# Prologue and first lots of a linear-attention and feed-forward kernel: another order of loads, scores and masks, narrower products of zeros, and the lower part of lot 4 placed sooner

## The chip, the cores and the metric

The kernel runs on one core of a Trainium2 chip. The metric is the device time of one execution in microseconds (us).

## The reference, cut to what matters

Linear attention with decay, in blocks of 64 tokens, over 4 batches, 8 heads, 768 tokens and 64 features; then a feed-forward network with a squared ReLU on the 3072 tokens of 512 features.

```python
for b in range(nb):
    qb, kb, vb = (q[:, :, sl], k[:, :, sl], v[:, :, sl])
    intra = np.einsum('bhic,bhjc->bhij', qb, kb) * Dmask[None]
    intra = np.einsum('bhij,bhjd->bhid', intra, vb)
    inter = np.einsum('bhid,bhde->bhie', qb * lam_pow[None], kv_state)
    out[:, :, sl] = intra + inter
    kv_state = lam_block * kv_state + np.einsum('bhsd,bhse->bhde', kb * rev_pow, vb)
...
h = x @ w_in
g = np.maximum(h, 0.0) ** 2
return g @ w_out
```

## The kernel before, in words

**Tiling.** Tokens are taken in 24 chunks of 128 (`t`), four of which make a group of 512 (`m`). For a chunk, `scores(t)` multiplies k and q of all heads into two PSUM tiles, `masked(t)` (VectorE, DVE) multiplies them with the decay mask into `a`, `news(t)`, `faded(t)` and `update(t)` carry the state `kv`, and `within(t)` and `before(t)` sum the chunk's output in PSUM. `split(t)` stores it as an upper part `xh` (ScalarE, ACT) and a lower part `xl` (DVE, the closure kept in `low[t]`). `prep_k(t)` and `prep_q(t)` scale k and q in place on GpSimd (POOL), with columns of the mask and with the powers `qpow`.

**Feed-forward.** For each of 16 slices `f` of the inner dimension, `hidden(m, f)` is 12 products into one PSUM bank: four of `wh` with `xh`, four of `wl` with `xh`, four of `wh` with `xl`. `square` (ACT) makes `gh`, `rest` (DVE) makes `gl`, and `project(m, f)` adds to four accumulators, for each of them a product of `gh` with `wh`, one of `gh` with `wl` and one of `gl` with `wh`. `project` of slice `f` is issued behind `hidden` of slice `f + 1`.

**Lots.** The weights come from memory as raw 64-bit words in 17 lots, counted from 0; lot `u` holds slice `u` of `w_in` and slice `u − 1` of `w_out`. A lot is loaded into `raw` (two buffers), then `first_hi(u)` (ACT) makes `A`, `first_lo(u)` (ACT) scales the low words in place, `clamp`, `shift`, `sign` and `rounded` (DVE) finish `A`, `upper(u)` (ACT) casts it to `wh`, and `lower(u)` (DVE) subtracts to `wl`. `A` too has two buffers. The load of lot `u + 2` waits until `rounded(u)` has read the buffer. `hidden(0, f)` needs lot `f`, `project(0, f)` lot `f + 1`. `turn` is a one-element copy on POOL that orders the work there.

**Order.** The order on each engine is written by hand: an engine runs its instructions as the program lists them. TensorE (PE) starts with products of zeros (L63 and L65, the second loop `PHASE = 7` products of 128 columns, each 2 records in the trace), then the masks' products (`get_mask`, L253), scores of chunk 0, the powers' products (`get_qpow`, L266), scores of chunk 1, and `news(0)`. The masks' products fill two banks of the pool `ps_h`; `halves[0]` (ACT) and `halves[1]` (DVE) copy them to the mask. Loads go through SyncE's queue (SP) in the order of the program; lot 2 through ACT's.

**The loop.** From `new_x(1)` on the loop over `f` issues, for each slice, `hidden(0, f)`, DVE's work on lot `f + 2`, `lower(f + 1)`, the load of lot `f + 4`, `square`, `rest`, ACT's work on lot `f + 3`, and one step of the attention of the next group: `scores(t)` at `f % 4 == 0`, `masked(t)` at 1, `attend(t)` (news, within, before, update, split) at 2.

Lines in the trace: L80 and L89 the loads of q, k and v; L115 the load of a lot; L120 `first_hi`; L125 `first_lo`; L133 `clamp`; L137 `shift`; L144 `sign`; L150 `rounded`; L156 `upper`; L159 `lower`; L259 the mask's copies; L285 `scores`; L298 `prep_k`; L292 `prep_q`; L304 `masked`; L319 `news`; L327 `within`; L334 `before`; L353 the addition to `kv`; L361 and L362 `xh` and `xl`; L523 `hidden`; L530 to L533 `square`; L538 `gl`; L553, L554 and L558 `project`.

Of the kernel before, what the change touches and what calls it, by code (L numbers as in the profile page):

```python
# [15 lines left out]
P = 128  # L16
# [9 lines left out]
G = 4  # L26
# [5 lines left out]
NLOT = NF + 1  # L32
# [3 lines left out]
def body(ctx: ExitStack, tc: tile.TileContext, qT, kT, kvq, lam, w, out):  # L36
    nc = tc.nc
# [5 lines left out]
    ps_acc = ctx.enter_context(tc.tile_pool(name="ps_acc", bufs=G, space=PSUM))  # L43
    ps_h = ctx.enter_context(tc.tile_pool(name="ps_h", bufs=2, space=PSUM))
# [11 lines left out]
    kv = const.tile([P, NPR, P], F32, name="kv")  # L56
# [4 lines left out]
    w_ = ps_a.tile([P, DM], F32, name="att")  # L61
    for n in (NPR, NPR, 2):
        nc.tensor.matmul(w_[:, 0 : n * P], kv[:, 0, :], kv[:, 0:n].rearrange("p a b -> p (a b)"), start=True, stop=True)  # L63
    for n in range(PHASE):
        nc.tensor.matmul(w_[:, 0:P], kv[:, 0, :], kv[:, 0, 0:P], start=True, stop=True)  # L65


    feat, tok, lent = {}, {}, {}
# [1 line left out]
    def load_qk(t):  # L70
        if t in (2, 3):
            lent[t] = wk.tile([P, 2, KT * C, 2], F32, name=f"lent{t}", tag=("xh", "xl")[t - 2])
            x = lent[t][:, 0].rearrange("p a b -> p (a b)")
        elif (t, 0) in lent:
            x = lent[t, 0]
        else:
            x = io.tile([P, 2 * DM], F32, name="qk_sb")
        feat[t] = x.rearrange("p (k a b) -> p k a b", k=2, a=NPR)
        for k, y in enumerate((kT, qT)):
            nc.sync.dma_start(out=feat[t][:, k], in_=y[t])  # L80

    def load_kv(t):
        if t in (2, 3):
            x = lent[t][:, 1].rearrange("p a b -> p (a b)")
        elif (t, 1) in lent:
            x = lent[t, 1]
        else:
            x = io.tile([P, 2 * DM], F32, name="kv_sb")
        nc.sync.dma_start(out=x, in_=kvq[t, :, 0 : 2 * DM])  # L89
        x = x.rearrange("p (k h d) -> p k h d", k=2, h=H)  # L90
        tok[t] = x[:, 0], x[:, 1]
# [8 lines left out]
    def lot(t, u):  # L100
        if u in (0, NF):
            return t[:, u : u + 1]
        return t.rearrange("p (s f) d -> p s f d", s=2)[:, :, u]

    def pieces(u):
        return [x for x in ((0, u), (1, u - 1)) if 0 <= x[1] < NF]
# [3 lines left out]
    def wload(u, engine=nc.sync):  # L110
        if u < NLOT:
            x = pieces(u)
            raw[u] = wk.tile([P, len(x) * DM], I64, name="raw", tag="raw")
            for i, (side, f) in enumerate(x):
                engine.dma_start(out=raw[u][:, i * DM : (i + 1) * DM], in_=w[side, :, f])  # L115
# [7 lines left out]
    def first_lo(u):  # L123
        L = cv[u][0]
        nc.scalar.activation(L, L, AF.Copy, scale=2.0**-29)  # L125

    def first(u):
        first_hi(u)
        first_lo(u)

    def clamp(u):
        A = cv[u][2].bitcast(F32)
        V.tensor_scalar(out=A, in0=A, scalar1=2.0**-15, scalar2=float(LIM), op0=ALU.max, op1=ALU.min)  # L133

    def shift(u):
        A = cv[u][2]
        V.tensor_scalar(  # L137
            out=A, in0=A, scalar1=3, scalar2=0x3FFFFFFF,
            op0=ALU.logical_shift_left, op1=ALU.bitwise_and,
        )  # L140

    def sign(u):
        L, Hw, A = cv[u]
        V.scalar_tensor_tensor(  # L144
            out=A, in0=Hw, scalar=0xC0000000, in1=A, op0=ALU.bitwise_and, op1=ALU.bitwise_or
        )

    def rounded(u):
        L, Hw, A = cv[u]
        V.tensor_tensor(out=A, in0=A, in1=L, op=ALU.add)  # L150

    def whole(u):
        return cv[u][2].bitcast(F32).rearrange("p (a d) -> p a d", d=DM)
# [4 lines left out]
    def lower(u):  # L158
        V.tensor_tensor(out=lot(wl, u), in0=whole(u), in1=lot(wh, u).bitcast(F32), op=ALU.subtract)  # L159
        cv.pop(u)  # L160

    def turn(u, half):
        x = cv[u][2].bitcast(F32)[0:1, 0:1] if half else wl[0:1, u, 0:1].bitcast(F32)
        nc.gpsimd.tensor_copy(mark[:, 0:1], x)

    wload(0)
    for t in (0, 1):
        load_qk(t)
        load_kv(t)
    load_qk(2)  # L170
    wload(1)
# [36 lines left out]
    for j in range(2):  # L208
# [5 lines left out]
        lambda o, x, y, op=op: V.tensor_tensor(out=o, in0=x, in1=y, op=op)  # L214
# [5 lines left out]
    b_, t_, u_, c_, d_, af = (sq[:, i, 0 : NS - 1] for i in range(6))  # L220
# [28 lines left out]
    def get_mask():  # L249
        half = [ps_h.tile([P, DM], F32, name="h") for _ in range(2)]  # L250
        nb = DM // P
        for b in range(2 * nb):
            nc.tensor.matmul(  # L253
                half[b // nb][:, b % nb * P : (b % nb + 1) * P], pz[:, b * T : b * T + C], one,
                start=True, stop=True, skip_group_check=True,
            )
        m = mask.rearrange("k j p (e b i) -> k (j p) e b i", e=2, i=T)
        return [
            lambda copy, e=e: copy(m[:, :, e], half[e].rearrange("k (b c i) -> k c b i", b=nb, i=T))  # L259
            for e in range(2)  # L260
        ]
# [18 lines left out]
    def scores(t, pool, name):  # L280
        sc_of[t] = [pool.tile([P, DM], F32, name=name) for _ in range(2)]
        k_, q_ = feat[t][:, 0], feat[t][:, 1]
        for p in range(NPR):
            for j, r in enumerate(rows):
                nc.tensor.matmul(  # L285
                    sc_of[t][j][:, p * C : (p + 1) * C], k_[r, p], q_[r, p],
                    start=True, stop=True, skip_group_check=True,
                )

    def prep_q(t):  # L290
        if t % NCB:
            nc.gpsimd.tensor_tensor(out=feat[t][:, 1], in0=feat[t][:, 1], in1=qpow, op=ALU.mult)  # L292
# [7 lines left out]
    def masked(t):  # L300
        a_of[t] = []
        for j in range(2):
            a = wk.tile([P, NPR, C], F32, name="a", tag="gl" if t in (1, 3) else "a")
            V.tensor_tensor(  # L304
                out=a, in0=sc_of[t][j].rearrange("p (a b) -> p a b", a=NPR),
                in1=mask[:, j], op=ALU.mult,
            )
            a_of[t].append(a)
# [267 lines left out]
    def new_x(m):  # L576
        xs_of[m] = [wk.tile([P, KT, N], F32R, name=n, tag=n) for n in ("xh", "xl")]
# [418 lines left out]


    new_x(0)
    halves = get_mask()
    first(0)  # L1000
    for op in (clamp, shift, sign):
# [1 line left out]
    halves[0](nc.scalar.copy)  # L1003
    halves[1](V.tensor_copy)
    rounded(0)
    scores(0, ps_acc, "acc")
    get_qpow()
    scores(1, ps_acc, "acc")
    prep_k(0)
    prep_k(1)  # L1010
    prep_q(1)
    masked(0)
    o, u, low = {}, {}, {}

    def att(t, pool, name):
# [9 lines left out]
    masked(1)  # L1025
    lower(0)
    first(1)
    scores(2, ps_h, "h")
    prep_q(2)
    prep_k(2)  # L1030
    att(1, ps_acc, "acc")
# [45 lines left out]
    for f in range(NF):  # L1077
        t, step, u_ = G + f // 4, f % 4, f + 2
        h = hidden(0, f, *xs_of[0])
        if f < 3:  # L1080
            if f < 2:
                lower(u_ - 1)
            clamp(u_)
            shift(u_)
            if f == 2:
                lower(u_ - 1)
            if f == 1:
                turn(u_, True)
                masked(t)
            sign(u_)  # L1090
            if f != 1:
                rounded(u_)
        else:
            if u_ < NLOT:
                for op in (clamp, shift, sign):
                    op(u_)
            if f > 3:
                upper(u_ - 1)
            lower(u_ - 1)
            if u_ - 1 < NF:  # L1100
                turn(u_ - 1, False)
            if u_ < NLOT:
                rounded(u_)
        wload(u_ + 2)
        if f == 3:
            low[G]()
        if f == 0:
            decay(3)
        if step == 0 and f or f == 1:
            prep_k(t)  # L1110
        if step == 1:
            prep_q(t)
        if step == 3:
            if t < 2 * G - 1:
                decay(t)
            else:
                fade_state(False)
        gh = square(h)
        rest(0, f, h, gh)
        if f == 1:  # L1120
            rounded(u_)
        if step == 1 and f > 1:
            masked(t)
        if f < 3:
            if f == 1:
                first_hi(u_ + 1)
            upper(u_)
            if f != 1:
                first_hi(u_ + 1)
        if step == 2:  # L1130
            low[t] = attend(t, ps_a, "att")
            if t > G:
                low[t]()
        if u_ + 1 < NLOT:
            if f >= 3:
                first_hi(u_ + 1)
            first_lo(u_ + 1)
        if prev is not None:
            project(*prev)
        prev = (0, f)  # L1140
        if step == 2:
            load_qk(t + 2)
            load_kv(t + 2)
        if step == 0:
            scores(t, ps_a, "att")
        if f == NF - 2:
            fold_mask()
            scale_k(t + 1)
        if f == NF - 1:
            open_half(t + 1)  # L1150
            scale_k(t + 2)
# [30 lines left out]
    for f in range(NF):  # L1182
        t = first_t + f // 2
        h = hidden(1, f, *xs_of[1])
# [53 lines left out]
    for f in range(NF):  # L1238
        t = first_t + f // 2
# [97 lines left out]
```

## Time and profile before

| what | value |
|---|---|
| time, median of 3 runs | 583.58 us (583.03 to 583.8) |
| time of the profiled execution | 583.46 us |
| its span, first to last instruction | 581.7 us |
| PE busy | 572.8 us, 98% of the span |
| DVE busy | 415.1 us, 71% |
| ACT busy | 272.4 us, 47% |
| POOL busy | 99.2 us, 17% |

The profile is one execution. Times in its rows are us from the start of the span; the time of the execution has 1.76 us more around the span. Busy shares are means over the whole span, and a stage can have another limit than the mean shows. A row of the time line gives start, busy time, engine, line, operation, output and inputs, and how many instructions it merges; in square brackets stands the idle time of the engine before it and what ended it.

### The profile page before, as it was taken

What the parts mean: (1) busy time and instruction counts of PE and PEld (TensorE: products, weight loads), DVE (VectorE), ACT (ScalarE), POOL (GpSimd) and SP (SyncE); (2) the same over time, 40 slices, a digit from 0 to 9 for tenths busy, and PEclk for the clock granted to TensorE, in tenths of its full rate; (3) what the DMA queues carried; (4) which work ended last, traced back from release to release, by engine and by line L of the source; (5) the groups of instructions that cost most, each with busy time, mean ns of one, the idle gap of its engine ahead of it and who ended that gap; (6) DMA issues with size and microseconds to landing.
All of it is one profiled execution on the core that took longest, in us unless ns stands there. A gap on an engine that the chain in (4) does not pass through costs nothing.

```text
span 581.7 us, 12568 instructions
## 1 busy us (share of the span) xinstructions
PE 572.8 (98%) x5020; PEld 485.6 (83%) x5020; DVE 415.1 (71%) x684; ACT 272.4 (47%) x501; POOL 99.2 (17%) x106
## 2 busy tenths in 40 slices
PE   9998999999999999999999999999999999999996
PEld 7986888888888888888888887888788888999996
DVE  5999999942788666786666668687645446997933
ACT  3777877725455556433333334444524234551510
POOL 4421222332322231000000013455000000000000
PEclk9999999999999999999999999999999999999999
DMA  8856576324689695566666645632297766776863
GB/s 300 333 176 242 157 277 217 111 74 145 223 294 373 226 302 181 173 193 198 197 199 199 199 162 168 233 116 71 77 322 231 191 194 186 246 215 204 287 206 106
DMA packets 69386, 119.32 MB, mean 205 GB/s; under 512 B 6352, under 2 KB 30928, under 8 KB 69328
## 3 DMA queue, kind: packets, MB, share of 16 engines
q1 hardware_dynamic: 66864, 115.37, 61.5%
q10 hardware_dynamic: 2464, 3.15, 1.5%
q8 instruction: 40, 0.66, 0.4%
q14 instruction: 18, 0.15, 0.1%
HBM read 88.08 MB, written 29.36 MB: 202 GB/s over the span
## 4 chain that ended last, share of the span: by engine, by line
PE 87%; DVE 8%; ACT 3%; issue 1%; DMA 0%; SPq 0%; DVEq 0%; POOL 0%; ACTq 0%; POOLq 0%
PE h L683 18%; PE h L523 12%; PE acc L553 9%; PE acc L558 8%; PE acc L554 8%; PE acc L931 8%; PE att L683 7%; PE att L931 4%; PE att L444 3%; PE h L931 2%; DVE sums L214 1%; PE h L411 1%; PE att L327 1%; PE att L63 1%; DVE rec L214 1%
## 5 line engine op out<-in xcount | busy, mean ns | idle before, releaser
L553 PE MATMUL acc<-wh,gh 128*128 128x512 f32 x256 | 101.1, 395 | 0.0
L558 PE MATMUL acc<-wh,gl 128*128 128x512 f32 x256 | 99.8, 390 | 0.0
L554 PE MATMUL acc<-wl,gh 128*128 128x512 f32 x256 | 99.8, 390 | 0.0
L683 PE MATMUL h<-wh,ring 128*128 128x512 f32 x320 | 85.8, 390 | 0.0
L530 ACT ACTIVATE h<-h 128x512 f32<-128x512 f32 x48 | 28.0, 583 | 103.6 <-PE h L523 45.8
L683 PEld LDWEIGHTS h<-wh,ring 128*128 128x128 f32 x320 | 59.9, 188 | 13.1 <-DVE kv_sb L214 0.4
L538 DVE TENSOR_TENSOR gl<-h,gh 128x512 fp32r<-128x512 f32 x48 | 32.9, 686 | 39.7 <-ACT h L533 39.7
L553 PEld LDWEIGHTS acc<-wh,gh 128*128 128x128 f32 x256 | 48.0, 188 | 10.9 <-issue 0.5
L558 PEld LDWEIGHTS acc<-wh,gl 128*128 128x128 f32 x256 | 48.1, 188 | 10.5 <-DVE gl L538 0.3
L554 PEld LDWEIGHTS acc<-wl,gh 128*128 128x128 f32 x256 | 48.1, 188 | 9.7
L683 PE MATMUL h<-wl,ring 128*128 128x512 f32 x160 | 49.3, 389 | 0.0
L395 POOL TENSOR_TENSOR kv_sb<-kv_sb,mask 128x512 f32<-128x512 f32 x13 | 16.0, 1229 | 126.0 <-DMA kv_sb<-in_kvq 125.9
L523 PE MATMUL h<-xh,wh 128*128 128x512 f32 x128 | 36.0, 403 | 0.5 <-DVE a L214 0.2
L523 PE MATMUL h<-xh,wl 128*128 128x512 f32 x128 | 34.5, 391 | 1.5 <-DVE wl L159 1.5
L512 POOL TENSOR_TENSOR kvd<-kv,qpow 128x256 f32<-128x256 f32 x27 | 22.3, 826 | 77.9 <-DVE kv L214 63.5
L683 PEld LDWEIGHTS h<-wl,ring 128*128 128x128 f32 x160 | 30.0, 188 | 6.3
L931 PE MATMUL acc<-folds,wh 128*128 128x256 f32 x192 | 35.2, 283 | 0.0
L523 PE MATMUL h<-xl,wh 128*128 128x512 f32 x128 | 34.2, 389 | 0.0
L683 PE MATMUL att<-wh,ring 128*128 128x512 f32 x128 | 34.2, 389 | 0.0
L214 DVE TENSOR_TENSOR wl<-sums,wh 128x1024 fp32r<-128x1024 f32 x24 | 29.2, 1218 | 1.9 <-ACT wh L903 1.9
L931 PEld LDWEIGHTS acc<-folds,wh 128*128 128x128 f32 x192 | 30.0, 192 | 0.0
L523 PEld LDWEIGHTS h<-xh,wl 128*128 128x128 f32 x128 | 23.9, 188 | 7.1 <-DVE wl L159 1.9
(253 smaller groups left out, 1197.0 us busy)
## 6 DMA issues: line engine op xcount, KB each, us to landing
ring<-ws SPq DMA_DIRECT2D x112, 256.0 KB, 3.0
folds<-wt SPq DMA_DIRECT2D x64, 256.0 KB, 3.7
raw<-in_w SPq DMA_DIRECT2D x30, 512.0 KB, 4.3
kv_sb<-in_kvq SPq DMA_DIRECT2D x19, 512.0 KB, 5.5
ws<-parts SPq DMA_DIRECT2D x32, 256.0 KB, 4.4
qk_sb<-in_kT SPq DMA_DIRECT2D x20, 256.0 KB, 4.2
qk_sb<-in_qT SPq DMA_DIRECT2D x20, 256.0 KB, 4.5
out_x<-o SPq DMA_DIRECT2D x16, 256.0 KB, 5.1
```

The lines of the kernel that those rows point to most:

```text
L214: lambda o, x, y, op=op: V.tensor_tensor(out=o, in0=x, in1=y, op=op)
L395: nc.gpsimd.tensor_tensor(out=x, in0=x, in1=y.broadcast_to([P, NPR, 2, D]), op=ALU.mult)
L444: nc.tensor.matmul(o[h][r, p * D : (p + 1) * D], x, y, start=(h, r.start) not in begun, stop=end, skip_group_check=True,)
L512: nc.gpsimd.tensor_tensor(out=kvd, in0=d, in1=qpow[:, :, D - 1 : D].broadcast_to([P, NPR, D]), op=ALU.mult)
L523: nc.tensor.matmul(h, wt[:, f, kt * P : (kt + 1) * P], x[:, kt], start=k == 0, stop=k == 11)
L530: nc.scalar.activation(h, h, AF.Relu)
L538: V.tensor_tensor(out=gl, in0=r, in1=gh.bitcast(F32), op=ALU.subtract)
L553: nc.tensor.matmul(accs[m][i], gh[:, cs], wh[:, j], start=f == 0, stop=False)
L554: nc.tensor.matmul(accs[m][i], gh[:, cs], wl[:, j], start=False, stop=False)
L558: nc.tensor.matmul(accs[m][i], gl[:, cs], wh[:, j], start=False, stop=end)
L683: nc.tensor.matmul(bank, x[:, part_, kt], t[:, q + kt], start=start and z == 0, stop=stop and z == 5, skip_group_check=True,)
L931: nc.tensor.matmul(bank[:, r * 2 * P : (r + 1) * 2 * P], x, y, start=n == 0 and r == 0 and z == 0, stop=n == NQ - 1 and z == 2, skip_group ...
```

## The change

The loads of k and q of chunks 0 and 1 go ahead of lot 0's. The seven products of zeros have 32 columns instead of 128. Scores of chunks 0 and 1 are issued ahead of the masks' products, scores of chunk 2 right behind `masked(0)` instead of behind `first(1)`. In the loop over `f`, `lower(4)` stands ahead of `clamp(5)` at `f = 3`; at `f = 4` and 5 `lower(f + 1)` stands ahead of `sign`; `rounded(5)` and `low[4]` stand behind `rest(0, 3)`; and `first_lo(6)` and `first_lo(7)` move from the end of slices 3 and 4 to the next slice, behind `upper`.

```diff
     for n in range(PHASE):
-        nc.tensor.matmul(w_[:, 0:P], kv[:, 0, :], kv[:, 0, 0:P], start=True, stop=True)
+        nc.tensor.matmul(w_[:, 0:32], kv[:, 0, :], kv[:, 0, 0:32], start=True, stop=True)
...
+    load_qk(0)
+    load_qk(1)
     wload(0)
     for t in (0, 1):
-        load_qk(t)
         load_kv(t)
     load_qk(2)
     wload(1)
...
     new_x(0)
+    scores(0, ps_acc, "acc")
+    scores(1, ps_acc, "acc")
     halves = get_mask()
     first(0)
...
     rounded(0)
-    scores(0, ps_acc, "acc")
     get_qpow()
-    scores(1, ps_acc, "acc")
     prep_k(0)
     prep_k(1)
     prep_q(1)
     masked(0)
+    scores(2, ps_h, "h")
...
     first(1)
-    scores(2, ps_h, "h")
...
         else:
-            if u_ < NLOT:
-                for op in (clamp, shift, sign):
-                    op(u_)
             if f > 3:
                 upper(u_ - 1)
-            lower(u_ - 1)
+                if f < 6:
+                    first_lo(u_)
+            if f == 3:
+                lower(u_ - 1)
+            if u_ < NLOT:
+                clamp(u_)
+                shift(u_)
+                if f in (4, 5):
+                    lower(u_ - 1)
+                sign(u_)
+            if f > 5:
+                lower(u_ - 1)
             if u_ - 1 < NF:
                 turn(u_ - 1, False)
-            if u_ < NLOT:
+            if u_ < NLOT and f > 3:
                 rounded(u_)
         wload(u_ + 2)
-        if f == 3:
-            low[G]()
...
         rest(0, f, h, gh)
-        if f == 1:
+        if f in (1, 3):
             rounded(u_)
+        if f == 3:
+            low[G]()
...
             if f >= 3:
                 first_hi(u_ + 1)
-            first_lo(u_ + 1)
+            if f not in (3, 4):
+                first_lo(u_ + 1)
```

## Rows read from the trace of the kernel before

**Rows 1.** The page's first part: busy time, share of the span and number of instructions of two engines.

```profile
PE 572.8 (98%) x5020; PEld 485.6 (83%) x5020; DVE 415.1 (71%) x684; ACT 272.4 (47%) x501; POOL 99.2 (17%) x106
```

**Rows 2.** The waits of PE and of its weight-load queue (PEld) over the whole span: engine and line, what they waited for, us in total, how often, the longest.

```profile
PE h L523 <- DVE wl L159: 1.5, 1, 1.5
...
PEld acc L558 <- DVE gl L538: 0.3, 1, 0.3
```

**Rows 3.** PE in order of time from 48.5 to 66 us: `hidden(0, 4)`, the start of the projection behind it, `hidden(0, 6)`, and `within(5)` (the last row's window ends before its last product).

```profile
48.56 1.07 PE L523 MATMUL h<-xh,wh 128*128 128x512 f32 x4
51.15 1.19 PE L523 MATMUL h<-xh,wl 128*128 128x512 f32 x4 [1.52 <-DVE wl L159]
...
53.10 0.39 PE L553 MATMUL acc<-wh,gh 128*128 128x512 f32 x1
...
62.80 1.07 PE L523 MATMUL h<-xh,wh 128*128 128x512 f32 x4
...
64.62 1.07 PE L523 MATMUL h<-xl,wh 128*128 128x512 f32 x4
65.61 0.65 PE L327 MATMUL att<-a,kv_sb 128*64 128x128 f32 x7
```

**Rows 4.** DVE in order of time from 45 to 66 us: the additions to `kv`, then `clamp(5)`, `lower(4)`, `rounded(5)`, `low[4]`, `gl(3)`, `clamp(6)`, `clamp(7)` and `masked(5)`.

```profile
45.66 0.86 DVE L353 TENSOR_TENSOR kv<-kvd,att 64x256 f32<-64x256 f32 x2
47.28 0.69 DVE L133 TENSOR_SCALAR A<-A 128x1024 f32<-128x1024 f32 x1 [0.76 <-ACT A L120]
...
49.88 1.22 DVE L159 TENSOR_TENSOR wl<-A,wh 128x1024 fp32r<-128x1024 f32 x1
51.02 1.22 DVE L150 CUSTOM_DVE_ANT_0 A<-raw,A 128x2048 uint16<-128x2048 uint16 x1
52.27 0.69 DVE L362 TENSOR_TENSOR xl<-att,xh 128x512 fp32r<-128x512 f32 x1
52.87 0.68 DVE L538 TENSOR_TENSOR gl<-h,gh 128x512 fp32r<-128x512 f32 x1
53.47 0.68 DVE L133 TENSOR_SCALAR A<-A 128x1024 f32<-128x1024 f32 x1
...
58.93 0.68 DVE L133 TENSOR_SCALAR A<-A 128x1024 f32<-128x1024 f32 x1
...
64.39 1.28 DVE L304 TENSOR_TENSOR a<-att,mask 128x512 f32<-128x512 f32 x2
```

**Rows 5.** First all waits of DVE from 47.3 to 120 us (columns as in rows 2; the 0.8 is the 0.76 of rows 4), then the busy time of each engine from 75 to 120 us (the second number is the stretch's length; at the end the clock, the DMA share and GB/s).

```profile
DVE A L133 <- ACT A L120: 1.2, 2, 0.8
...
75.00:120.00 45.00, 45.00 (x281) 36.65 (x281) 43.97 (x55) 34.21 (x46) 14.15 (x15) 1.00 0.53 178
```

**Rows 6.** ACT in order of time from 45 to 66 us: `upper(4)`, `first_hi(5)`, the last step of `square` of slice 3, and `first_hi(7)`.

```profile
45.18 1.05 ACT L156 CAST wh<-A 128x1024 fp32r<-128x1024 f32 x1 [1.25 <-DVE A L150]
46.13 1.12 ACT L120 ACTIVATE A<-raw 128x1024 f32<-128x1024 f32 x1
...
49.79 0.59 ACT L533 ACTIVATE h<-h 128x512 f32<-128x512 f32 x1
...
57.35 1.17 ACT L120 ACTIVATE A<-raw 128x1024 f32<-128x1024 f32 x1 [1.48 <-DVE wl L159]
```

**Rows 7.** The load issued between 52.6 and 52.8 us, the second half of lot 7: its size and us from issue to landing.

```profile
raw<-in_w SPq DMA_DIRECT2D x1, 512.0 KB, 4.6
```

**Rows 8.** PE at the start: the first product of zeros and the second record; then the records of the seven products, in three windows (from the first one on, from 6.87 on, from 7.69 on: the number behind x falls as the window begins later); last, from the list of instructions on `qk_sb`, the score products with the least, median and greatest ns of one.

```profile
1.38 1.22 PE L63 MATMUL att<-kv 128*128 128x512 f32 x1 [1.38 <-POOL pz L189]
...
2.39 1.06 PE L63 MATMUL att<-kv 128*128 128x512 f32 x1
...
5.81 2.38 PE L65 MATMUL att<-kv 128*128 128x128 f32 x14
...
6.87 1.31 PE L65 MATMUL att<-kv 128*128 128x128 f32 x9
...
7.69 0.50 PE L65 MATMUL att<-kv 128*128 128x128 f32 x3
...
L285 PE MATMUL acc<-qk_sb x32: 272/272/373, 9.9 to 13.0; 64*128 64x128 f32 x32
```

**Rows 9.** The prologue. PE in order of time: masks' products, scores of chunk 0, powers' products, `news(0)`. Then the busy time of each engine (PE, PEld, DVE, ACT, POOL) from DVE's mask copy at 10.01 to `lower(1)` at 26.16; the two `prep_k` on POOL (least, median and greatest ns); and two loads with us from issue to landing: q of chunk 0, issued between 2.6 and 2.7 us, and the second half of lot 2, issued by ACT at 18.4.

```profile
8.02 1.95 PE L253 MATMUL h<-pz 128*128 128x128 f32 x16
9.90 1.16 PE L285 MATMUL acc<-qk_sb 64*128 64x128 f32 x16
10.99 1.15 PE L266 MATMUL att<-pz,odd 8*128 8x128 f32 x8
...
13.17 0.69 PE L319 MATMUL att<-kv_sb 128*64 128x64 f32 x16
...
10.01:26.16 16.15, 16.15 (x299) 14.99 (x300) 13.92 (x19) 9.75 (x20) 9.13 (x7) 1.00 0.91 346
...
L298 POOL TENSOR_TENSOR kv_sb<-kv_sb,mask x2: 1051/1241/1431, 10.8 to 12.2; 128x512 f32<-128x512 f32 x2
...
qk_sb<-in_qT SPq DMA_DIRECT2D x1, 256.0 KB, 4.4
...
raw<-in_w ACTq DMA_DIRECT2D x1, 512.0 KB, 6.8
```

## The prediction

> **What bounds the kernel now.** I read the page first: PE is busy 572.8 us of the 581.7 us span, DVE 415.1 [rows 1]. With one engine busy 98% of the time, the first question is where it is not. The waits of PE over the whole execution answer it: apart from the start, the one long wait is 1.5 us for `wl` (L159), with 0.3 us for `gl` (L538) next to it in the weight-load queue [rows 2]. The third view is PE in order of time around that wait. `hidden(0, 4)` begins at 48.56; its second third, the first to read `wl`, follows at 51.15, and the projection behind it at 53.10. So the product lasts 4.54 us, where `hidden(0, 6)` needs 64.62 − 62.80 = 1.82 for two thirds, so 2.72 for three [rows 3]. The stall costs 1.82 us. With 0.2 to 0.3 for `gl` behind it, some 2.05 us is the most that the fifth lot (lot 4, counted from 0) can give back.
>
> A wait of PE says only what came last. What decides is what set that producer's time, and here a fourth view is needed: DVE between 45 and 66 us [rows 4]. DVE idles 0.76 us before `clamp(5)` at 47.28, for the A that ACT makes. From there to 120 us it waits just twice, 1.2 us together [rows 5]: it runs its list without a break, `lower(4)` at 49.88, `rounded(5)` at 51.02, and so on to `masked(5)` at 64.39. That last entry is the one to look at: it takes 1.28 us for two halves, ending at 65.67, and `within(5)` on PE starts at 65.61 [rows 3, 4], when `hidden(0, 6)` has just run out (64.62 + 0.91 = 65.53). So 14 us after the stall PE is again exactly level with DVE. A gain of PE that DVE does not share ends there.
>
> **Lot 4's lower part sooner.** The change puts `lower(4)` ahead of `clamp(5)`, `shift(5)`, `sign(5)`. No instruction is removed. Its operand `wh` is cast by 45.18 + 1.05 = 46.23 [rows 6] and DVE is free at 45.66 + 0.86 = 46.52 [rows 4], so it starts at 46.52 and ends near 47.7; PE wants it at 48.56 + 0.91 = 49.47. Both stalls of PE go: `gl(3)` also moves ahead of `rounded(5)` and is ready near 51.1, where PE wants it about 51.8.
>
> Now DVE's list, by the starts of rows 4. `lower(4)` takes 1.14 (49.88 to 51.02), so `clamp(5)` starts at 47.66; clamp, shift and sign take 2.60 (47.28 to 49.88) and end at 50.26. `gl(3)` must wait for ACT's square, 49.79 + 0.59 = 50.38 [rows 6]; it starts at 50.42 and takes 0.60. `rounded(5)` starts at 51.02, the very time of before; `low[4]` follows at 52.27, as before, and `clamp(6)` at 52.87, where `gl(3)` stood, against 53.47. DVE is 0.60 ahead: the 0.76 idle is filled, 0.16 of a new wait comes. One lot on there is a second loss. The load of lot 7 waits for `rounded(5)`, which has not moved, and its second half is issued between 52.6 and 52.7 and takes 4.6 us [rows 7], so it lands near 57.23; ACT's A(7) then ends at 57.23 + 1.17 = 58.40 [rows 6], and `clamp(7)`, free to start at 58.33, starts at 58.47 against 58.93. DVE is 0.46 ahead. Within `f = 4` and `f = 5` the same five instructions per lot run in another order, which moves nothing past them; `first_lo(6)`, moved behind `upper(5)` on ACT, ends near 54.4, before `rounded(6)` at 56.6. So `masked(5)` starts at 63.93 and its second half ends at 65.21. PE, free of its stalls, would be there at 65.61 − 2.05 = 63.56, and waits: of 2.05 it keeps **0.46**. The bounds: 0.76 if neither wait comes (all of the idle time that there is), 0.2 if ACT, which now casts `upper(5)` and makes L(6) ahead of the squares of `f = 4`, delays `gl(4)` by another 0.3. From `f = 6` on the order of both engines is that of before, with DVE busy 43.97 of 45.00 us from 75 to 120 [rows 5], so I carry 0.46 to the end.
>
> **Zeros' products of 32 columns.** Seven products are 14 records on PE, from 5.81 to 8.02 [rows 8]. [...] Fewer columns shorten the product, not the weight load of 128 columns ahead of each. What a load costs uncovered, the rows show twice: the first product lasts 1.22 where the next lasts 1.06, so 0.16 at the lower level; the first score product lasts 0.373 where the others last 0.272, so 0.10 at the higher. If the loads set the pace, 1.35 us at 0.16 make 8.4 records and the other 5.6 at 0.105 take 0.6: the end comes at 7.76, **0.25 sooner**. Bounds: nothing, if load and product don't overlap (0.16 + 0.05 is today's 0.21); 1.46, if only columns count (14 × 0.053 = 0.75 instead of 2.21). I take 0.25, the value of the two measured loads; were a load as quick at the lower level as at the higher, 14 × 0.105 = 1.47 would save 0.74, a rival below. [...]
>
> **The prologue in another order.** The same products run in the order scores 0, scores 1, masks, powers, scores 2, `news(0)`. PE's work up to `news(0)` is 1.09 longer (9.90 to 10.99, one set of scores [rows 9]) and that after it 1.09 shorter, so by itself nothing. The loads hide: the fourth transfer of before, q of chunk 0, was issued at about 2.65 and took 4.4 us [rows 9], so 1 MB was there by 7.05; k and q of two chunks are that megabyte, and the first scores come at 7.8. Lot 0 lands near 8.6 (512 KB more at 346 GB/s [rows 9]); its steps on ACT and DVE, half as wide as lot 5's 1.12 and 2.60, end near 10.5 by that estimate, and the mask copy behind them on DVE waits for PE until 12.2 anyway. What is late next: that copy moves from 10.01 to 12.2 (two sets of scores), so POOL's `prep_k(0)` starts at 12.97 and, at 1.43 [rows 9], ends at 14.40; PE wants it at 13.17 + 1.09 = 14.26 [rows 9]. **0.2** lost with the semaphore, behind which all of PE stands. DVE has 13.92 us of work in the 16.15 from the copy to `lower(1)` at 26.16 [rows 9]. Begun at 12.2, with some 0.3 left of its 2.2 us of waits (the first `xh`, which ACT makes behind the powers, 1.1 later), it ends at 26.3 to 26.5, in step with PE's 0.2. ACT's queue also issues the load of lot 2, behind the same list: it landed near 25.2 (18.4 + 6.8 [rows 9]) and would land near 26.2, just as ACT takes it up, behind the cast that `lower(1)` waits for. On SP the k, q of both chunks pass lot 0 and kv of chunk 0, nothing else. Bounds: 0, if `prep_k` takes the 1.05 of its other row; 0.6, if DVE slips by a further 0.4. All these times shift by what the zeros save.
>
> **Sum.** −0.46 − 0.25 + 0.2 = −0.51. The profiled execution took 583.46 (581.7 span and 1.76 around it), 0.12 under the median of 583.58: **582.9**, own range 582.2 to 583.6.
>
> **The rivals.**
> - *PE keeps everything* (2.05 + 0.25 − 0.2 = 2.1): 581.4. For it: PE's own listing. Against: the sum of DVE's work, which can't reach `masked(5)` more than 0.76 sooner. It needs DVE instructions to become shorter, for instance by meeting POOL's less. 0.15.
> - *Loads are as quick at the lower level* (0.74): 0.46 + 0.74 − 0.2 = 1.0, so 582.5. For it: the 0.10 of the higher level. Against: the 0.16 measured at the lower. 0.10.
> - *Thin products save by columns* (1.46): 0.46 + 1.46 − 0.2 = 1.7, so 581.7. For it: products of 128 columns do keep pace with columns. Against: the 0.16. 0.10.
> - *The prologue gives it back*: POOL and DVE late by 0.6, nothing from the zeros, 0.2 from lot 4: 583.9. The change then does not do what it says. 0.13.
> - *Slower: the clock.* [...] 0.08. [...]
>
> **Chances.** Forecast 0.44, the others as given. A measurement of this kernel tells about 0.2%, 1.17 us, from no change: faster is below 582.4, slower above 584.75. Faster: the first and the third rival, 0.04 of the second and 0.02 of the forecast, 0.31. Slower: the clock and 0.01 of the prologue's, 0.09. Same 0.60. Range for 8 in 10: 581.3 to 584.4.
>
> **What would show it.** `lower(4)` before 48, no wait of `hidden(0, 4)`, and a new wait of PE of about 1.6 us ahead of `within(5)` (L327) for DVE's `masked(5)`; without that wait the forecast is wrong. In the zeros, records at 0.16 and 0.105; at 0.05 the second rival holds. A spacing of 0.21 in the scores is the clock. A wait of `news(0)` (L319) on POOL is the 0.2.

## The result and the profile after

The changed kernel took 586.81 us (median of 12 runs, 586.03 to 591.39) against 583.84 (12 runs, 582.65 to 585.42) of the kernel before on the same chip: ratio 1.0060, 95% interval 1.0039 to 1.0081. It is slower by some 3 us, outside the forecast range of 581.3 to 584.4. Two of the twelve (590.89 and 591.39) stand 3.5 us above the next; the profile is of the first of these.

The page's first part of the changed kernel, and then its waits of PE (engine and line, what it waited for, us in total, how often, the longest):

```profile
span 589.2 us, 12565 instructions
PE 578.3 (98%) x5020; PEld 490.2 (83%) x5020; DVE 418.3 (71%) x684; ACT 272.5 (46%) x501; POOL 98.0 (17%) x106
```

```profile
PE att L328 <- DVE a L305: 2.4, 2, 2.2
...
PE acc L328 <- DVE a L305: 0.8, 2, 0.7
```

The 1.5 us for `wl` of [rows 2] are gone, and 2.2 us for `masked(5)` stand in their place (lines are one higher than before; the 0.8 lies in the prologue, behind the late start described next). PE was also busy 5.5 us longer than in [rows 1], with the same 5020 products, so products themselves took longer. PE in order of time shows where. First the start, then `hidden(0, 6)`, `within(5)`, `before(5)` and the first steps of the projection:

```profile
5.81 3.03 PE L65 MATMUL att<-kv 128*128 128x32 f32 x14
8.77 3.79 PE L286 MATMUL acc<-qk_sb 64*128 64x128 f32 x32
12.49 2.72 PE L254 MATMUL h<-pz 128*128 128x128 f32 x16
...
65.55 1.07 PE L524 MATMUL h<-xh,wh 128*128 128x512 f32 x4
...
67.36 1.07 PE L524 MATMUL h<-xl,wh 128*128 128x512 f32 x4
70.63 0.43 PE L328 MATMUL att<-a,kv_sb 128*64 128x128 f32 x2 [2.19 <-DVE a L305]
...
72.13 2.11 PE L335 MATMUL att<-qk_sb,kv 128*64 128x128 f32 x15
74.17 0.80 PE L554 MATMUL acc<-wh,gh 128*128 128x512 f32 x1
...
75.51 0.39 PE L554 MATMUL acc<-wh,gh 128*128 128x512 f32 x1
```

The 14 thin records take 2.96 us, 0.21 apart, and two sets of scores 3.72, where the one set of [rows 9] took 1.09. From 13.9 on the masks' products lie 0.11 apart and not 0.21: up to there PE ran at half speed, which before, by the spacing in [rows 8] (0.21 up to 6.87, 0.11 from 7.69 on), ended at about 7.2. These two speeds are the lower and the higher level of the prediction. Only the spacing shows them at the start; the clock column of the windows has 1.00 there in both kernels, from 5.8 to 8 us before and from 6 to 16 after. And behind the wait of 2.19 us the products run at half speed again, here with 0.50 in the clock column, from 71.95 to 75.36: 2.11 us for 15 of `before(5)` (1.14 in e9), 0.80 for a product of the projection, back at 0.39 from 75.51. DVE from `lower(4)` to `masked(5)`; this execution stands 4.59 us late here because of its start, which has to be taken off to compare with [rows 4]:

```profile
51.22 1.23 DVE L159 TENSOR_TENSOR wl<-A,wh 128x1024 fp32r<-128x1024 f32 x1
52.36 0.69 DVE L133 TENSOR_SCALAR A<-A 128x1024 f32<-128x1024 f32 x1
...
55.72 1.22 DVE L150 CUSTOM_DVE_ANT_0 A<-raw,A 128x2048 uint16<-128x2048 uint16 x1
...
57.45 0.68 DVE L133 TENSOR_SCALAR A<-A 128x1024 f32<-128x1024 f32 x1
...
61.27 1.23 DVE L150 CUSTOM_DVE_ANT_0 A<-raw,A 128x2048 uint16<-128x2048 uint16 x1
...
63.31 0.69 DVE L133 TENSOR_SCALAR A<-A 128x1024 f32<-128x1024 f32 x1 [0.21 <-ACT A L120]
...
64.65 1.22 DVE L159 TENSOR_TENSOR wl<-A,wh 128x1024 fp32r<-128x1024 f32 x1
65.79 1.22 DVE L144 SCALAR_TENSOR_TENSOR A<-raw,A 128x1024 uint32<-128x1024 uint32 x1
67.14 2.23 DVE L150 CUSTOM_DVE_ANT_0 A<-raw,A 128x2048 uint16<-128x2048 uint16 x1
69.30 0.68 DVE L539 TENSOR_TENSOR gl<-h,gh 128x512 fp32r<-128x512 f32 x1
69.90 1.27 DVE L305 TENSOR_TENSOR a<-att,mask 128x512 f32<-128x512 f32 x2
```

The row to look at is `rounded(7)` at 67.14: 2.23 us, where `rounded(5)` took 1.22 and `rounded(6)`, at 61.27, 1.23. `rounded(6)` stands behind a pair that was swapped in the same way, `lower(5)` ahead of `sign(6)`, so the swap alone doesn't make it long. POOL beside it, in the changed kernel (`turn(6)` and `prep_q(5)`):

```profile
66.00 1.04 POOL L164 COPY mark<-wl 1x1 f32<-1x1 f32 x1 [4.83 <-DVE wl L159]
67.00 1.28 POOL L293 TENSOR_TENSOR qk_sb<-qk_sb,qpow 128x512 f32<-128x512 f32 x1
```

and the same two in the kernel before, where `rounded(7)` ran from 62.65 to 63.87 and `gl(5)` and `masked(5)` behind it:

```profile
62.86 1.04 POOL L164 COPY mark<-wl 1x1 f32<-1x1 f32 x1 [4.41 <-DVE wl L159]
63.87 1.29 POOL L292 TENSOR_TENSOR qk_sb<-qk_sb,qpow 128x512 f32<-128x512 f32 x1
```

`turn(6)` waits for `lower(6)` and copies one element, yet it ends with the DVE instruction that runs beside it: before with `rounded(7)`, after with `sign(7)` (65.79 + 1.22 = 67.01). Then `prep_q(5)` starts, and after the change `rounded(7)` is what it meets: it begins at 67.14, `prep_q` ends at 68.28, and from there to 69.37 is 1.09, about one undisturbed `rounded`. Before, `prep_q(5)` met `gl(5)` and `masked(5)`, which read PSUM and kept their 0.68 and 1.28 [rows 4].

### The profile page after: what moved, and what is told of

It is laid out like the page before. It is cut to its first block, busy times and chain, and to the rows that moved or that the text cites. A ratio compares the mean times of both kernels' runs of the same rounds, so it can differ in the third digit from the quotient of the medians.

```text
span 589.2 us, 12565 instructions
## 1 busy us (share of the span) xinstructions
PE 578.3 (98%) x5020; PEld 490.2 (83%) x5020; DVE 418.3 (71%) x684; ACT 272.5 (46%) x501; POOL 98.0 (17%) x106
## 4 chain that ended last, share of the span: by engine, by line
PE 76%; DVE 10%; DMA 6%; ACT 4%; issue 2%; SPq 1%; POOL 0%; DVEq 0%; ACTq 0%; POOLq 0%
PE h L684 18%; PE h L524 9%; PE acc L554 8%; PE acc L932 7%; PE acc L555 7%; PE acc L559 7%; PE att L684 7%; PE att L932 4%; PE att L445 2%; PE h L932 2%; DMA lent<-in_kvq 1%; DMA raw<-in_w 1%; DVE sums L215 1%; DVE A L150 1%; DVE A L144 1%
## 5 line engine op out<-in xcount | busy, mean ns | idle before, releaser
L533 ACT ACTIVATE gh<-h 128x512 fp32r<-128x512 f32 x48 | 28.8, 600 | 1.5
```

The costliest lines, as they stand in the source:

```text
L533: nc.scalar.activation(gh, h, AF.Square)
```

## The experiments

Every ratio is to the kernel before on the same chip, where its median was 583.94 to 584.09. The table shows how far PE's start of some blocks lies from that of the kernel before in each profiled execution (us, from PE in order of time; a rise between `hidden(0, 6)` and `hidden(0, 7)` is what `within(5)` and the clock behind it cost):

| block | before | after | e1 | e3 | e6 | e9 | e10 | e12 |
|---|---|---|---|---|---|---|---|---|
| `news(0)` | 13.17 | +4.34 | +1.04 | −0.23 | +0.80 | −0.80 | +1.28 | −0.66 |
| `hidden(0, 0)` | 25.42 | +4.57 | −0.10 | −0.23 | +0.86 | +0.23 | +0.15 | +0.31 |
| `hidden(0, 4)` | 48.56 | +4.59 | −0.09 | −0.23 | +0.80 | +0.21 | +0.21 | +0.27 |
| `hidden(0, 5)` | 57.23 | +2.54 | −2.14 | −2.27 | −1.24 | −1.84 | −1.83 | −1.77 |
| `hidden(0, 6)` | 62.80 | +2.75 | −1.93 | −2.17 | −1.01 | −1.68 | −1.66 | −1.60 |
| `hidden(0, 7)` | 70.50 | +7.09 | +2.29 | +0.60 | −1.15 | −0.09 | +2.62 | −0.60 |
| `hidden(0, 9)` | 82.57 | +7.09 | +2.29 | +0.60 | +0.80 | −0.09 | +2.62 | −0.60 |

**The parts alone.** e1: the changed kernel with the zeros' products at 128 columns again. e2: only the thin products. e3: only the loop over `f`. e4: only the order of loads, scores and masks.

```diff
 e1, against after; e2 is the reverse, against before
-        nc.tensor.matmul(w_[:, 0:32], kv[:, 0, :], kv[:, 0, 0:32], start=True, stop=True)
+        nc.tensor.matmul(w_[:, 0:P], kv[:, 0, :], kv[:, 0, 0:P], start=True, stop=True)
```

> The changed kernel with the seven products of zeros at 128 columns again; all else as changed. Theory A, the thin products keep TensorE at its lower clock until about 13.9 us: with wide ones the records of the zeros go from 0.21 to 0.11 apart near 7.2, the scores run at 0.11 a record, and the time is the forecast's sum without the zeros, 0.46 - 0.2 = 0.3 us under the kernel before (583.5). Theory B, the new order of loads and scores itself makes the prologue late (POOL, DVE, the loads of kv and of the lots): the zeros change little and the time stays near 586.8.

> The kernel before with nothing changed but the seven products of zeros, 32 columns instead of 128. Theory A: the clock rises near 13.9 us, the masks' products and scores run at 0.21 a record, and the time is 2.5 to 4 us over the kernel before (586.3 to 587.8). Theory B: no change beyond 0.3 us (583.5 to 584.1).

> The kernel before with the loop's part of the change alone (lower(4) ahead of clamp(5), and what moves with it). My reading of DVE as the bound: hidden(0,4) no longer waits, TensorE waits about 1.6 us for masked(5) ahead of within(5) instead, and 0.46 us are kept (583.3 to 583.4 where before is 583.8). Rival, TensorE keeps all: 2.05 us (581.8) and no new wait. A third way: the new wait of TensorE, 1.6 to 2.2 us, lowers the clock, as the changed kernel's profile shows near 72 us; then the time is about 1.2 us over the kernel before (585.0).

> The kernel before with the new order of loads, scores and masks alone, the zeros at 128 columns and the loop as before. Theory A: 0.0 to 0.6 us slower, 0.2 by the forecast's sum (584.0), with a wait of news(0) for prep_k(0). Theory B: 2 us slower or more.

e1: 586.32, ratio 1.0034 (1.0021 to 1.0046). e2: 583.82, 0.9999 (0.9985 to 1.0012). e3: 585.51, 1.0020 (1.0007 to 1.0032). e4: 584.49, 1.0004 (0.9993 to 1.0015). So the thin products show no saving (the interval is −0.9 to +0.7 us), the prologue no clear loss (−0.4 to +0.9), and the loop by itself loses some 1.2 us. With wide zeros the whole change is 1.5 us better than with thin ones (1.0034 against 1.0060), but the two intervals overlap, and e2 has no loss to match. DVE, and then PE, of e3:

```profile
62.26 2.24 DVE L150 CUSTOM_DVE_ANT_0 A<-raw,A 128x2048 uint16<-128x2048 uint16 x1
...
65.03 1.27 DVE L304 TENSOR_TENSOR a<-att,mask 128x512 f32<-128x512 f32 x2
```

```profile
65.76 0.43 PE L327 MATMUL att<-a,kv_sb 128*64 128x128 f32 x2 [2.24 <-DVE a L304]
```

The long `rounded(7)` is there without the prologue, `masked(5)` starts 0.64 later than in [rows 4], and the 2.05 us that PE had gained by `hidden(0, 5)` (from −0.23 to −2.27) are lost, with 0.83 more, at `hidden(0, 7)`. In e2 and e4 PE waits in the prologue for the transfer of q, which the list of before does not have: in both for q of chunk 3 (the tile `acc`), in e4 also for q of chunk 2 (the tile `h`), whose scores the new order puts ahead of `news(0)`. The wait for chunk 3 belongs to neither part of the change: e9, below, has it too, with the prologue of before (e2, e4, e9):

```profile
PE acc L285 <- DMA lent<-in_qT: 1.1, 1, 1.1
```

```profile
PE h L286 <- DMA lent<-in_qT: 0.6, 1, 0.6
PE acc L286 <- DMA lent<-in_qT: 0.5, 1, 0.5
```

```profile
PE acc L285 <- DMA lent<-in_qT: 1.0, 1, 1.0
```

**Lot 6 as before.** e5 is the changed kernel, e9 the loop part alone, both with `lower(6)` behind `sign(7)` again; lots 4 and 5 stay as changed.

```diff
-                if f in (4, 5):
+                if f == 4:
                     lower(u_ - 1)
                 sign(u_)
-            if f > 5:
+            if f > 4:
                 lower(u_ - 1)
```

> The changed kernel with lower(6) behind sign(7) again, as in the kernel before (slice 5 only). Theory C, POOL's prep_q(5) follows turn(6), which follows lower(6); with lower(6) moved sooner prep_q(5) falls on rounded(7), which took 2.23 instead of 1.22 us: now rounded(7) takes 1.22, masked(5) is 1.0 us sooner, and within(5) waits 1.1 to 1.3 us instead of 2.2. If the shorter wait leaves the clock up, 1.0 + 1.7 us are saved (584 to 584.5 where the changed kernel is 586.6); if the clock falls all the same, 1.0 (585.6). Rival, POOL has no part in it: rounded(7) stays at 2.2 and the time at 586.6.

> The kernel before (own prologue, zeros of 128 columns) with the loop's part of the change, but lower(6) behind sign(7) as before. It is the forecast's step by itself, without the meeting of prep_q(5) and rounded(7). Theory C: rounded(7) takes 1.2 us, masked(5) comes 0.3 to 0.5 us sooner than in the kernel before, within(5) waits 1.5 to 1.7 us for it, and from slice 7 on TensorE is 0.3 to 0.5 us ahead, so 583.5 where before is 583.9; a fall of the clock in the wait, if it comes, adds 1.6. Rival: DVE is late by another cause, and slice 7 starts 0.5 us or more later than in the kernel before, as in the run with the whole loop part (0.8).

e5: 584.24, 1.0015 (0.9997 to 1.0033); its profiled execution took 1365.78 us, so its rows are not compared with the others. e9: 583.95, 0.9999 (0.9988 to 1.0010). The one swap of `lower(6)` and `sign(7)` is worth 2.6 us in the changed kernel (1.0060 against 1.0015) and 1.2 in the loop part alone (1.0020 against 0.9999; these two intervals just overlap, the first two don't). DVE, POOL and PE of e9:

```profile
62.60 1.22 DVE L150 CUSTOM_DVE_ANT_0 A<-raw,A 128x2048 uint16<-128x2048 uint16 x1
...
64.33 1.28 DVE L304 TENSOR_TENSOR a<-att,mask 128x512 f32<-128x512 f32 x2
```

```profile
63.82 1.30 POOL L292 TENSOR_TENSOR qk_sb<-qk_sb,qpow 128x512 f32<-128x512 f32 x1
```

```profile
62.74 1.20 PE L523 MATMUL h<-xh,wl 128*128 128x512 f32 x4 [0.54 <-DVE wl L159]
...
65.07 0.43 PE L327 MATMUL att<-a,kv_sb 128*64 128x128 f32 x2 [0.21 <-DVE a L304]
```

`prep_q(5)` falls on `gl(5)` and `masked(5)` again, `rounded(7)` is short again. PE now waits for `lower(6)` instead, then for `masked(5)`: of 2.05 us it keeps 0.30 (+0.21 to −0.09). The wait of 1.5 to 1.7 us that was expected for `within(5)` is split between the two.

**The wait and the clock.** e10 is the changed kernel once more. e8 and e11 put eight products of 512 columns, whose result is not used, into PE's list: e8 ahead of `within(5)`, e11 ahead of `hidden(0, 6)`.

```diff
 e8, in within(t)
+        for n in range(8 if t == G + 1 else 0):
+            nc.tensor.matmul(u, wh[:, 0, 0:P], xs_of[0][0][:, n % KT], start=True, stop=True)
 e11, in hidden(m, f)
+        for n in range(8 if (m, f) == (0, 6) else 0):
+            nc.tensor.matmul(h, wh[:, f, 0:P], xh[:, n % KT], start=True, stop=True)
```

> The changed kernel with 8 products of 512 columns (0.23 us each, 1.8 us in all) into an unused PSUM tile, issued ahead of within(5), so that TensorE works through most of its wait for masked(5); they add work that no output needs. Theory, a good part of the loss is the clock that falls in the wait: masked(5) and within(5) come at the same time as in the changed kernel, the clock is 0.999 instead of 0.996 and the time 1.5 to 1.7 us less (585.0). Rival, the clock has no part in it and the wait alone costs: the time is that of the changed kernel (586.6) or up to 0.3 more.

> The changed kernel once more, for the profile of another execution. Theory: the clock that rises at 14 us and costs 4.5 us belongs to few executions (2 of 12 times stood near 591, the rest near 586.4). In this one the clock rises between 5 and 8 us, hidden(0,0) starts within 0.5 us of the kernel before, and falls in the wait of within(5): 586.4. Rival: the late rise is the rule, hidden(0,0) starts 4 us late, 590.

> The changed kernel with 8 more products of 512 columns (1.8 us) at the head of hidden(0,6), into its own bank, which the true products then overwrite. TensorE has that work while DVE goes on to masked(5), so it waits 0.3 to 0.6 us there instead of 2.2; within(5) comes at the same time. Theory, the clock falls in the long wait and this costs 1.6: no fall, 584.7 to 585.0. Rival, the fall has nothing to do with the wait or costs nothing: 586.4, as the changed kernel, or more by what these products displace.

e8: 587.33, 1.0056 (1.0042 to 1.0070). It does not test the filling of the wait: its products write a bank that `masked(5)` still reads, so they waited as `within(5)` had (2.2 us) and came on top. e10: 587.35, 1.0064 (1.0040 to 1.0088). e11: 585.72, 1.0029 (1.0015 to 1.0042). With some 1.8 us more work for PE, e11 is 1.6 us faster than the same kernel without it, e10, on the same chip (585.0 at most was expected); its `hidden(0, 7)` starts 0.66 us later than before, that of e10 2.62. What differs is the wait and, behind it, the granted clock (third number from the end). The stretch behind the wait in after, e1, e10, e11 and e3 (each stretch with its length, then busy time of PE, PEld, DVE, ACT, POOL, clock, DMA share, GB/s):

```profile
71.95:75.36 3.41, 3.41 (x25) 2.90 (x22) 3.38 (x4) 1.14 (x3) 0.33 (x1) 0.50 0.52 210
```

```profile
67.08:70.49 3.41, 3.41 (x25) 2.88 (x22) 3.38 (x4) 1.55 (x4) 0.28 (x1) 0.50 0.54 219
```

```profile
66.63:70.04 3.41, 3.25 (x30) 3.20 (x30) 3.34 (x5) 1.39 (x3) 0.00 (x0) 0.50 0.74 287
```

```profile
66.00:71.00 5.00, 4.83 (x44) 3.96 (x44) 4.93 (x6) 2.88 (x5) 0.78 (x1) 1.00 0.52 195
```

```profile
65.80:71.00 5.20, 5.03 (x44) 4.16 (x45) 5.13 (x6) 3.08 (x5) 0.84 (x1) 1.00 0.53 193
```

The wait of PE for `masked` in e11:

```profile
PE att L328 <- DVE a L305: 0.5, 2, 0.4
```

Three times PE's granted clock is 0.50 for 3.41 us behind its wait, which costs half of that, 1.7 us; in e11, which has a wait of 0.4 us there, it is 1.00. But the wait does not always bring the fall: the profiled executions of e3 (2.24; 1.00 from 65.8 to 71) and e8 (2.2; mean clock 0.999) have it and no fall. The times of e3 split accordingly: six of its twelve have a mean clock of 0.995 to 0.997 and take 586.25 us on average, six have 0.998 or more and take 584.34. All 12 of the changed kernel are at 0.995 to 0.997, all 31 of before beside e3 and all 12 of e11 at 0.998 or more. The mean clock is a rough sign, though: one execution of e4, which has no wait of 2 us, is at 0.996, and one of before beside e5 at 0.948, neither of them slow for it (584.76 and 584.41).

**`masked` sooner.** e6 is the changed kernel, e7 the loop part alone, with `masked` of slices 5, 9 and 13 moved right behind `lower`; these are chunks 5, 6 and 7, and where the expectations write `masked(9)` and `masked(13)` they mean the slices. e12 is e9 with them behind `rounded` and ahead of `gl`.

```diff
 e6, e7
                 if f in (4, 5):
                     lower(u_ - 1)
+                if f == 5:
+                    masked(t)
                 sign(u_)
             if f > 5:
                 lower(u_ - 1)
+                if step == 1:
+                    masked(t)
...
-        if step == 1 and f > 1:
-            masked(t)
 e12, against e9
             if u_ < NLOT and f > 3:
                 rounded(u_)
+        if step == 1 and f > 1:
+            masked(t)
...
         rest(0, f, h, gh)
...
-        if step == 1 and f > 1:
-            masked(t)
```

> The changed kernel with masked(5), masked(9) and masked(13) sooner in DVE's list, behind lower of their slice instead of behind gl: masked(5) ends near 62.5, about 1 us before TensorE wants it. Theory, the wait of within(5) and the fall of the clock in it are the whole loss of the loop: no wait there, clock 0.999, and 2.0 us under the kernel before but for 0.3 to 0.5 of the prologue (582.3 to 582.5 where before is 583.9). Rival, the clock falls for another reason or DVE is the bound at another place behind: the time stays over 584, with another wait of TensorE between 66 and 120 us.

> The kernel before, its own prologue and zeros of 128 columns, with the loop's part of the change and masked(5), masked(9), masked(13) sooner. Theory as for the run before it: 1.8 to 2.05 us under the kernel before (581.9 to 582.1), no wait of hidden(0,4) and none of within(5). Rival: as there, 583.5 or more. Against the run before it this tells what the prologue's part costs with the loop mended: 0.3 to 0.5 us by the forecast's sum, nothing by its own comparison (1.0004).

> The run with lower(6) late and the prologue of before, with masked(5), masked(9), masked(13) directly ahead of gl of their slice (behind rounded, so no load of a lot waits for it). Theory, DVE sets the end and only the place of masked(5) in its list counts: masked(5) 0.6 sooner again, within(5) waits 0.9 to 1.1 us, TensorE keeps 0.9 to 1.1 from slice 7 on and the clock stays up: 582.9 where before is 583.9. Rival, as with masked behind lower: the gain is taken back at slices 8 to 13 by waits for wl, 583.9.

e6: 584.87, 1.0021 (1.0006 to 1.0037). e7: 584.53, 1.0012 (1.0003 to 1.0021). Both were expected 1.4 to 2.0 us under the kernel before; their rival, DVE as the bound at a place behind, came instead. e12: 583.26, 0.9985 (0.9976 to 0.9994), the only version faster than the kernel before (582.9 was expected). In e6 the wait of `within(5)` and the fall are gone and PE is 1.95 us ahead of its place at `hidden(0, 4)` when `hidden(0, 7)` starts; at `hidden(0, 9)` all of it is gone. DVE, POOL, ACT and PE of e6:

```profile
61.94 1.28 DVE L305 TENSOR_TENSOR a<-att,mask 128x512 f32<-128x512 f32 x2
63.14 1.52 DVE L144 SCALAR_TENSOR_TENSOR A<-raw,A 128x1024 uint32<-128x1024 uint32 x1
64.79 1.23 DVE L150 CUSTOM_DVE_ANT_0 A<-raw,A 128x2048 uint16<-128x2048 uint16 x1
...
73.64 0.69 DVE L133 TENSOR_SCALAR A<-A 128x1024 f32<-128x1024 f32 x1 [0.96 <-ACT A L120]
```

```profile
62.15 0.18 POOL L164 COPY mark<-wl 1x1 f32<-1x1 f32 x1 [4.78 <-DVE wl L159]
62.29 1.29 POOL L293 TENSOR_TENSOR qk_sb<-qk_sb,qpow 128x512 f32<-128x512 f32 x1
```

```profile
72.49 1.12 ACT L120 ACTIVATE A<-raw 128x1024 f32<-128x1024 f32 x1 [3.27 <-DMA raw<-in_w]
```

```profile
75.64 1.19 PE L524 MATMUL h<-xh,wh 128*128 128x512 f32 x4 [0.42 <-ACT wh L156]
...
77.52 1.19 PE L524 MATMUL h<-xh,wl 128*128 128x512 f32 x4 [0.68 <-DVE wl L159]
```

`masked(5)`, and with 0.3 us a `sign(7)` that `prep_q(5)` now meets, push `rounded(7)` to 64.79, from 62.65 before (0.80 of the difference stood already at `hidden(0, 4)`); the load of lot 9 waits for `rounded(7)`, ACT waits 3.27 us for that load, DVE 0.96 for ACT, and PE 0.42 and 0.68 for `upper(8)` and `lower(8)`. In e12 `rounded(7)` keeps its place and what `masked` pushes is `gl(5)`. DVE and PE of e12:

```profile
62.65 1.22 DVE L150 CUSTOM_DVE_ANT_0 A<-raw,A 128x2048 uint16<-128x2048 uint16 x1
63.78 1.28 DVE L304 TENSOR_TENSOR a<-att,mask 128x512 f32<-128x512 f32 x2
```

```profile
64.82 1.28 PE L327 MATMUL att<-a,kv_sb 128*64 128x128 f32 x15
```

PE enters `within(5)` without a wait and keeps 0.87 us (+0.27 to −0.60) to the end.

## Why the prediction was wrong

**The bound was right.** That PE would be stopped at `within(5)` by DVE is what every profile with the loop part shows, except where `masked` was moved (2.1 to 2.2 us in most of them, 0.2 in e9, 0.4 in e11). With 4.59 taken off, `clamp(5)` starts at 47.77 (forecast 47.66), `rounded(5)` at 51.13 (51.02), `clamp(6)` at 52.86 (52.87), `clamp(7)` at 58.72 behind the forecast wait for ACT (58.47). Without the swap of lot 6, e9 keeps 0.30 us of 2.05, where the sum said 0.46 and gave 0.2 as its lower bound.

**The step that failed** is the sentence that within `f = 4` and `f = 5` "the same five instructions per lot run in another order, which moves nothing past them". It looked at DVE's list alone. Behind `lower(6)` stand `turn(6)` and `prep_q(5)` on POOL, so these moved too, from `gl(5)` and `masked(5)` onto `rounded(7)`, which took 1.01 us longer. `masked(5)` came 0.64 later than before (e3) and not 0.46 sooner. That this swap is the cause is shown by e5 and e9, which undo nothing else: both are faster for it, and in the rows of e9 `rounded(7)` is back at 1.22. It could have been read in the trace of before: a copy of one element that takes 1.04 us there, and ends with the DVE instruction beside it, hints that one of the two waits for the other. The first rival spoke of DVE meeting POOL less; meeting it more was not priced.

**The second part of the loss**, 1.7 us, no step had: the wait that I forecast and costed as time only (1.6 us; it was 2.2) also lowered PE's granted clock, to 0.50 for 3.41 us. That PE's idle time has a part in it is shown by e11, where work in its place leaves the clock up (1.00 from 66 to 71, a mean of 0.998 or more in all twelve executions) and wins 1.6 us net of its own cost; that it is not enough is shown by the profiles of e3 and e8. Before, the 1.5 us wait for `wl` [rows 2] had no such fall, by the mean clock, in those 31 executions (1.00 from 51.2 to 56 in the profiled one). Why e3 has the fall in half of its executions and the changed kernel in all of them stays open.

**The zeros** were forecast to give 0.25; e2 shows 0.0, with an interval that holds the 0.25 too. The rows speak for the lower bound, nothing. The term that failed is the load of 0.16 at the lower level, taken for 1.35 us, from 5.81 to about 7.16. No run shows a record at 0.16: at that level 32 columns take 0.21 us (after), just as 128 did [rows 8], and one weight load takes 0.33 to 0.34 us beside either width. Whether load and product add up to that or the load alone takes it, no run separates. Nor did the 1.35 us hold: all 14 records of after stand at the lower level, all 14 of e2 at the higher, where they take 1.48 us (5.68 to 7.16), 0.106 each, where the forecast had 0.105 and 128 columns had 0.11 [rows 8]; so there is next to nothing to save at either level. PE of e2:

```profile
5.68 1.65 PE L65 MATMUL att<-kv 128*128 128x32 f32 x14
7.16 2.03 PE L253 MATMUL h<-pz 128*128 128x128 f32 x16
```

And what is gained ahead of the scores does not reach the feed-forward network: `news(0)` started from 0.80 sooner (e9) to 1.28 later (e10), `hidden(0, 0)` 0.23 and 0.15 later. In e2 `news(0)` starts 0.79 sooner, PE then waits 1.1 us for q, and `hidden(0, 0)` starts 0.35 later. That "all these times shift by what the zeros save" was thus wrong too.

**The prologue's order** was forecast to cost 0.2. e4 alone shows 0.2 (1.0004), with an interval of −0.4 to +0.9; e5 against e9, which differ in the zeros too, shows 0.9, and their intervals overlap. The forecast wait did not come: in e4 the list of PE's waits has no wait of `news(0)` for `prep_k(0)`, but 0.6 us for q of chunk 2, and 0.5 for q of chunk 3, a wait that e9 has with the order of before. At `hidden(0, 0)` the six profiles with the new order, without the one with the late start, lie from −0.22 (e11) to +0.86 (e6), the six with the old from −0.23 (e3) to +0.35 (e2, e7). Whether the order costs anything is open.

**The slower rival** named the clock. In the profiled execution the change from half to full speed did come late, at 13.9 against about 7.2, and cost 4.3 us at `news(0)`. But only two of the twelve executions stand that high, and e2, with the same thin products, has an unchanged median. So the late rise makes a tail and not the median, and that the median came out slower, as this rival had it, is chance. One or two executions 2.2 to 3.9 us above the next one are found in e2, e5, e6, e10 and e11, all with thin products (e8, thin as well, has none in six); of the versions with 128 columns only e9 has one, 2.1 above. That thin products cause the tail is likely from these counts and not shown, since no second profile caught one.

**The sum again.** By the ratios the swap of lot 6 accounts for 2.6 us of the 3.5 that 1.0060 stands for (3.0 by the medians). The rows agree: from `hidden(0, 4)` to `hidden(0, 7)`, 1.1 from the collision (0.83 lost in e3, 0.30 kept in e9) and 1.7 from the clock make 2.8, and e10 against e9 has 2.7. The rest, 0.9 by the ratios, no run assigns: the intervals of e2 and e4, up to +0.7 and +0.9, leave room for it and for nothing.

## What to carry to other kernels

When an instruction moves, follow everything that waits for it on every engine, helpers of one element too, and ask what their new neighbours are: on DVE and POOL a neighbour can nearly double an instruction (1.22 to 2.23 us here). A wait on TensorE can cost more than its length, since the clock may fall behind it (1.7 us behind 2.2); here even unneeded work in its place was cheaper. And a gain on one engine lasts only to the place where the next engine is level, so that engine's list has to be reordered in the same change, as in e12, without delaying what releases a load.

## What the runs showed of the hardware

- **DVE and POOL lengthen some of each other's instructions.** POOL's copy of one element takes 1.04 us beside `sign` or `rounded`, 0.18 beside `masked` (e6, at 62.15), and DVE's `rounded` 2.23 instead of 1.22 beside a `prep_q` of 1.28 (2.23 to 2.24 in after and e3). In e6 `sign(7)`, begun at 63.14 with `prep_q(5)` still running to 63.58, takes 1.52 instead of 1.22. The instructions of DVE that read PSUM (`gl` 0.68, `masked` 1.28) and the `prep_q` of 1.29 beside them keep their lengths. In after `rounded(7)` ends 1.09 us behind the end of `prep_q(5)` (68.28 to 69.37), about one whole `rounded`, as if it had waited for that end; why, no run shows.
- **PE's granted clock** fell from 1.00 to 0.50 behind a wait of 2.1 to 2.2 us in the midst of dense work, in three of the five profiled executions that had it (after, e1 and e10, not e3 and e8). Where it fell it stayed down for 3.41 us.
- **PE's full speed at the start**, by the spacing of its products, was there by 5.52 us in e4 (14 records of 128 columns in 1.66 us from there on, 0.12 each) and by 5.68 in e2 (14 of 32 columns in 1.48), came at about 7.2 before and at 13.9 in after, in profiles of nearly the same start; a difference of some us at a kernel's start can be that alone (4.34 at `news(0)` of after).
